# A long convolution with an MLP: three chunks of the next pass on GpSimd, raw weights ten steps ahead, the decay on the filter's first layer, MLP tiles moved

## The chip, the cores and the metric

The kernel runs on one core of a Trainium2 chip. The metric is the device time of one execution in microseconds, and of several runs the median. The engines appear under the profile's names: PE (TensorE: matmuls; its weight loads have a row of their own, PEld), DVE (VectorE), ACT (ScalarE), POOL (GpSimd) and SP (SyncE, which only issues DMAs here). Each engine executes its own instructions in the order in which they were issued to it; so does the queue of DMA issues of SP, and that of POOL. An instruction that waits holds up all that stand behind it on its engine.

## The reference

A long convolution of length 12480 (by FFT of twice the length) of u = x * v with a learned filter, gated by x, and then an MLP with a squared ReLU over all 49920 tokens.

```python
# x, v: (4, 12480, 128); pos_emb: (12480, 64); w1: (64, 64); w2: (64, 128); float32
h_filt = (np.maximum(pos_emb @ w1, 0.0) @ w2) * np.exp(-0.01 * pos)[:, None]
u = x * v
y = np.fft.irfft(np.fft.rfft(u, n=2*S, axis=1) * np.fft.rfft(h_filt, n=2*S, axis=0)[None], n=2*S, axis=1)[:, :S]
t = (x * y).reshape(B * S, D)                      # 49920 tokens of 128
r = np.maximum(t @ moe_w_in, 0.0)                  # (128, 2048), float64
out = ((r * r) @ moe_w_out).astype(np.float32)     # (2048, 128), float64
```

The decay exp(-0.01 * pos) underflows to zero beyond some thousands of positions, so the kernel computes only RF = 96 rows of 128 filter positions.

## The kernel before

The transform is done as two stages of matmuls with matrices of cosines and sines (sizes N1 = 90 and N2 = 128). The 128 channels are worked on in Q = 4 passes of 32 channels and all four batches. A pass `q` has two loops.

*First transforms* (`for c in range(NC)`, 20 steps). A chunk is 8 columns out of batch x channel. Chunks 0 to 15 carry data: `load_c` fetches x and v as [98, 1024] tiles (lines 164 to 168), `prep(c)` makes u on DVE from one product and an addition and a subtraction (lines 180 and 183). Chunks 16 to 19 carry the filter, which is fetched from DRAM tile `fd` and copied into u by ACT (line 189). `s1_quad` then does the matmuls of half a chunk (line 199) into one of two PSUM buffers, and ACT copies the result into the big SBUF tile P (line 202). In step c the kernel issues in this order: the load of chunk c + 5, the next piece of the weight conversion, in pass 0 the filter's layers, `prep(c + 2)`, and the two `s1_quad(c, .)`.

*The weight conversion.* The MLP's weights arrive as float64. `weights(i)` is a generator that handles one of eight column blocks: it fetches 512 KB of raw words into a single buffer (line 231), converts them by integer arithmetic on DVE into a high and a low float32 part (lines 237 to 256, 13 DVE instructions on 128x512 and an ACT copy) and stores them to DRAM tile `wd` (line 258). Each `next(part, 0)` runs it on to its next `yield`. A block is begun at steps 0 and 10 of each pass, so its raw load is issued one step ahead of the instructions that read it.

*The filter* (pass 0, steps 0 to 7; two pairs of groups a step). `filt(i)` is the first layer: a matmul of pos with w1 and a ReLU on ACT (line 134). `filt2(i)` is the second: 16 matmuls (line 143), a product with the decay on DVE (line 147, out of PSUM), then an addition on DVE and a subtraction on POOL (line 156) into the two `feo` tiles, of which there is one buffer each. `store_f` writes them to `fd` at the end of the step.

*Second transforms* (`for s in range(NS)`, 30 steps). `s2(z)` multiplies P with matrices `wt` that are fetched from DRAM, three steps ahead by `load_s(z + 3)` (lines 264 and 276). ACT copies the filter's part (line 280), DVE multiplies (line 284, PSUM by SBUF), POOL combines the products into y (lines 292 and 293). `i2(z - 2)`, two steps later, applies the inverse of the second stage to y (line 301); ACT and DVE take it out of PSUM and SP stores it to `cd` in DRAM (line 307). The list `todo` holds the transforms whose `i2` is outstanding: two are left at the end of the loop, and line 368 executes them after the first transforms of the next pass. Near the end of the loop (steps 24, 26, 28) the first three chunks of the next pass are loaded, and at steps 26 and 28 two of them prepared on DVE.

SBUF buffers: x, the products t and half of the filter tiles share five buffers with the tag "x"; v, y, the results `cs` and the other half of the filter tiles share five with the tag "v". u has four.

*The MLP stage* begins with `load3(0)` and `load3(1)`, which fetch a unit's columns of `cd`, its x and its inverse matrices (lines 395 to 405). `i1` does the inverse first stage, `tr` gates and transposes, and `h_chunk`, `g_chunk` and `o_chunk` do the two layers with weights split in high and low parts (`wi`, `wo`). `wi` and `w0` (the first unit's matrices) are fetched at the beginning of the last pass's second transforms, `wo` between `load3(0)` and `load3(1)`. The order of all instructions is the order of the program text (`tc.manual_schedule()`); the framework adds the waits that the data and the buffers need.

## Time and profile before

| | us |
|---|---|
| runs: median (lowest, highest) of 3 | 3218.98 (3217.07, 3224.23) |
| the profiled execution: its time | 3214.31 |
| the profiled execution: its span | 3212.4 |
| PE busy | 3037.3 (95%) |
| DVE busy | 2383.7 (74%) |
| ACT busy | 2107.2 (66%) |
| POOL busy | 704.1 (22%) |
| granted TensorE clock, mean | 0.977 |
| DMA, mean over the span | 91 GB/s |

The span is the part of the execution that the profile covers. An engine's busy time counts its instructions, not its waits. A row of the timeline has the start in us from the beginning of the span, the duration, the engine, the line, the operation with its output and inputs, and in brackets the idle time ahead of it and what ended that; SPq and POOLq are the queues of DMA issues. A row of the windows has a stretch, its length, the busy time of each engine with its number of instructions, the granted TensorE clock, the mean busy share of the 16 DMA engines and what they moved in GB/s.

### The profile page before, as it was taken

How to read it: one execution, taken by the hardware profiler on the slowest of the kernel's cores; microseconds unless marked ns; L12 is line 12 of the kernel's file. 1: busy time of each engine (PE TensorE's matmuls, PEld its weight loads, DVE VectorE, ACT ScalarE, POOL GpSimd, SP SyncE). 2: the span in 40 equal slices, each digit the busy share in tenths (PEclk: the TensorE clock that was granted, in tenths of full speed). 3: DMA queues.
4: the chain of work that ended last, by engine and by line, in shares of the span. 5: the costliest groups of instructions: out<-in, count | busy, mean ns of one | idle time of the engine just before them, and what ended most of it. 6: DMA issues, size and time to landing. Idle time of an engine off the chain costs nothing.

```text
span 3212.4 us, 41665 instructions
## 1 busy us (share of the span) xinstructions
PE 3037.3 (95%) x15338; PEld 2448.3 (76%) x15338; DVE 2383.7 (74%) x2765; ACT 2107.2 (66%) x2658; POOL 704.1 (22%) x598
## 2 busy tenths in 40 slices
PE   7696977879799999999999999999999999999999
PEld 4575766667688888888888888888888888888887
DVE  6596776759577777777777777777777777777776
ACT  2433434243577777777777777777777777777776
POOL 3160523406211112111111111111111111111210
PEclk8898989899899999999999999999999999999999
DMA  7576574766512122121122121222121221121200
GB/s 213 134 210 199 158 231 131 221 178 185 146 56 58 51 73 63 51 57 57 51 75 58 55 58 58 60 62 66 51 58 51 62 69 56 58 58 51 65 28 14
DMA packets 204266, 291.78 MB, mean 91 GB/s; under 512 B 13278, under 2 KB 129568, under 8 KB 203552
## 3 DMA queue, kind: packets, MB, share of 16 engines
q1 hardware_dynamic: 194704, 263.04, 28.6%
q0 software_dynamic: 9360, 26.10, 3.1%
q8 instruction: 121, 1.98, 0.3%
q14 instruction: 81, 0.66, 0.1%
HBM read 205.85 MB, written 83.23 MB: 90 GB/s over the span
## 4 chain that ended last, share of the span: by engine, by line
PE 85%; DMA 6%; DVE 6%; ACT 2%; issue 1%; POOL 0%; SPq 0%; DVEq 0%; POOLq 0%; ACTq 0%
PE psh L470 34%; PE pso L496 34%; PE psx L276 5%; PE psy L439 4%; PE psc L301 4%; DVE x L180 2%; DVE u L183 1%; PE pst L456 1%; PE pss L199 1%; DMA f<-fd 1%; DMA raw<-in_w_out_dram 1%; ACT u L189 1%; DMA cb<-cd 1%; DMA wt<-in_sw_dram 1%; DVE t L284 1%
## 5 line engine op out<-in xcount | busy, mean ns | idle before, releaser
L88 DVE TENSOR_TENSOR glo<-gt,ghi 128x1024 fp32r<-128x1024 f32 (+1 forms) x784 | 1090.2, 1390 | 60.6 <-PE psh L470 0.9
L473 ACT ACTIVATE rt<-psh 128x1024 f32<-128x1024 f32 (+1 forms) x784 | 800.0, 1020 | 433.7 <-PE psh L470 424.5
L482 DVE CAST ghi<-gt 128x1024 fp32r<-128x1024 f32 (+1 forms) x784 | 540.4, 689 | 502.9 <-ACT gt L480 502.4
L496 PE MATMUL pso<-ghi,wo 128*128 128x512 f32 (+1 forms) x3136 | 871.4, 395 | 0.0
L470 PE MATMUL psh<-xhi,wi 128*128 128x512 f32 (+1 forms) x3136 | 867.0, 398 | 0.9 <-ACT rt L473 0.4
L480 ACT ACTIVATE gt<-rt 128x1024 f32<-128x1024 f32 (+1 forms) x784 | 829.1, 1058 | 23.7 <-DVE glo L88 0.4
L496 PEld LDWEIGHTS pso<-ghi,wo 128*128 128x128 f32 x3136 | 591.2, 189 | 134.7
L470 PEld LDWEIGHTS psh<-xhi,wi 128*128 128x128 f32 x3136 | 579.9, 188 | 130.3 <-ACT rt L473 1.3
L88 POOL TENSOR_TENSOR clo<-ca,chi 128x512 fp32r<-128x512 f32 x126 | 225.1, 1787 | 1391.8 <-ACT chi L85 1369.1
L496 PE MATMUL pso<-glo,wo 128*128 128x512 f32 (+1 forms) x1568 | 504.8, 393 | 0.0
L470 PE MATMUL psh<-xlo,wi 128*128 128x512 f32 (+1 forms) x1568 | 488.8, 393 | 0.0
L199 PE MATMUL pss<-e_sb,u 98*64 98x180 f32 (+1 forms) x2560 | 249.7, 350 | 107.0 <-DVE u L183 84.6
L496 PEld LDWEIGHTS pso<-glo,wo 128*128 128x128 f32 x1568 | 294.9, 188 | 70.5
L470 PEld LDWEIGHTS psh<-xlo,wi 128*128 128x128 f32 x1568 | 294.8, 188 | 69.9
L199 PEld LDWEIGHTS pss<-e_sb,u 98*64 98x64 f32 (+1 forms) x2560 | 212.3, 152 | 143.7 <-issue 86.7
L202 ACT COPY P<-pss 128x720 f32<-128x720 f32 x160 | 125.2, 794 | 229.8 <-PE pss L199 229.8
L284 DVE TENSOR_TENSOR t<-psx,hs 128x768 f32<-128x768 f32 x240 | 218.2, 952 | 49.8 <-ACT hs L280 28.7
L276 PEld LDWEIGHTS psx<-P,wt 128*128 128x128 f32 x1440 | 212.5, 188 | 46.8 <-issue 11.7
L276 PE MATMUL psx<-P,wt 128*128 128x160 f32 x1440 | 221.9, 302 | 14.0 <-DMA wt<-in_sw_dram 6.6
L280 ACT COPY hs<-psx 128x192 f32<-128x192 f32 x240 | 65.1, 323 | 237.2 <-PE psx L276 233.8
L292 POOL TENSOR_TENSOR y<-t,t 128x384 f32<-128x384 f32 x120 | 120.3, 1002 | 377.2 <-DVE t L284 371.5
L88 POOL TENSOR_TENSOR clo<-cb,chi 104x512 fp32r<-104x512 f32 x126 | 165.8, 1316 | 114.1 <-ACT chi L85 114.0
(58 smaller groups left out, 1964.4 us busy)
## 6 DMA issues: line engine op xcount, KB each, us to landing
cd<-cs SPq DMA_DIRECT2D x120, 384.0 KB
cb<-cd SPq DMA_DIRECT2D x128, 208.0 KB
x<-in_xc_dram SPq DMA_DIRECT2D x64, 392.0 KB
v<-in_vc_dram SPq DMA_DIRECT2D x64, 392.0 KB
x<-in_x_dram SPq DMA_DIRECT2D x128, 196.0 KB
iwt<-in_iw_dram POOLq DMA_DIRECT2D x63, 392.0 KB, 3.4
out_dram<-os SPq DMA_DIRECT2D x48, 512.0 KB
wt<-in_sw_dram SPq DMA_DIRECT2D x120, 192.0 KB
```

What stands on the lines that cost most here:

```text
L88: eng.tensor_tensor(dst, src, hi.bitcast(F32), op=ALU.subtract)
L199: pe.matmul(pv[p, a], lhsT=u[:rows, 4 * h + a, p], rhs=e_sb[:rows, e : e + 2].rearrange("n c k -> n (c k)"), start=True, stop=True)
L202: act.copy(sl["P"][:, :, s : s + 4].rearrange("p m a t -> p a m t"), pv.rearrange("p a (m t) -> p a m t", t=2),)
L276: pe.matmul(xp[:, 3 * c + i, :SIG], lhsT=wt[:, i], rhs=sl["P"][:, c * (N1 // 2) + kp, :, t], start=True, stop=True)
L284: dve.tensor_tensor(t, xp[:, :, : B * QC].rearrange("p m (b d) -> p m b d", b=B), hs[:, c].rearrange("p r k d -> p (r k) d").unsqueeze(2). ...
L301: pe.matmul(cp[c], lhsT=f_sb[:, c], rhs=y[:, c], start=True, stop=True)
L439: pe.matmul(yp, lhsT=lhs, rhs=rhs, start=n == 0, stop=n == len(ops) - 1)
L470: pe.matmul(ps[:, j, :n], lhsT=wi[wp][:, f * 128 : (f + 1) * 128], rhs=bl[b][dp][:, j * n : (j + 1) * n], start=(wp, dp) == TERMS[0], stop ...
L473: act.activation(rt, ps[:, :, :n], AF.Relu)
L480: act.activation(gt, rt, AF.Square)
L482: dve.tensor_copy(hi, gt)
L496: pe.matmul(un["o"][j], lhsT=wo[tm[0]][:, f], rhs=g[tm[1]][:, j], start=f == 0 and tm == TERMS[0], stop=f == NF - 1 and tm == TERMS[-1])
```

## The change

1. *Chunks 0 to 2 of the next pass.* A new function `ahead` loads x and v into two buffers of its own (`a0`, `a1`, one each) and makes u on POOL in four instructions: two halves of the product, the addition, the subtraction. Its five parts run at every second step of the second transforms, beginning at steps 2, 10 and 18, in passes 0 to 2. The first transforms of passes 1 to 3 then begin with three chunks ready, and DVE prepares chunks 3 to 15.
2. *Raw weights.* The raw load is issued from POOL's queue instead of SP's, at step 9 of the first transforms for the block that begins at step 10, and before the loops or at step 16 of the second transforms for the block that begins at step 0. The conversion runs at steps 0 to 6 and 10 to 16, and the store at steps 9 and 19.
3. *Leftover `i2`.* The two outstanding transforms run in steps 1 and 2 of the next first transforms instead of behind them.
4. *Filter chunks.* Half of the copies into u go to DVE.
5. *Decay.* It is fetched together with pos, repeated over the 64 inner rows, and multiplied in with the ReLU in one DVE instruction; addition and subtraction follow on the first layer's output (DVE), and ACT copies the second layer's results out of PSUM into `feo`. POOL has no part in the filter any more.
6. *MLP tiles.* `wi`, `w0` and `wo` are fetched at steps 2, 6, 10 and 14 of the last pass's second transforms; the identity matrix is fetched at the beginning. A pad of 992 words moves addresses of the MLP stage, and the tile of constants is longer.

```diff
 load_f:
-                pt = wf.tile([2 * FO, G2 * RF], F32, tag="pos", name="pt", bufs=3)
+                pt = wf.tile([2 * FO, 2, G2 * RF], F32, tag="pos", name="pt", bufs=3)
 filt:
+            pt = sf.pop(("pos", i))
+            pe.matmul(ps, lhsT=w1_sb, rhs=pt[:, 0], start=True, stop=True)
+            hw = pt[:, 1]
+            dve.scalar_tensor_tensor(hw, ps, 0.0, hw, op0=ALU.max, op1=ALU.mult)
             h1 = wf.tile([2 * FO, G2, RF], F32, tag="h1", name="h1")
-            act.activation(h1.rearrange("p a b -> p (a b)"), ps, AF.Relu)
+            for e, op in enumerate((ALU.add, ALU.subtract)):
+                dve.tensor_tensor(h1[:, 2 * e : 2 * e + 2].rearrange("p a b -> p (a b)"),
+                                  hw[:, : 2 * RF], hw[:, 2 * RF :], op=op)
 filt2:
-                dve.tensor_tensor(ft, ps[h], win_sb[...], op=ALU.mult)
-                for e, op in enumerate((ALU.add, ALU.subtract)):
-                    (dve, pool)[e].tensor_tensor(fe, ft[:, :2], ft[:, 2:], op=op)
+                for e in range(2):
+                    act.copy(fe, ps[h][:, 2 * e : 2 * e + 2].rearrange("p j (q d) -> p j q d", q=Q))
 prep, filter chunks:
-                for e in range(2):
+                for e, copy in enumerate((dve.tensor_copy, act.copy)):
                     for h in range(2):
-                        act.copy(u[:RF, :, j : j + 32], ch["f", e, h][:, d : d + 8])
+                        copy(u[:RF, :, j : j + 32], ch["f", e, h][:, d : d + 8])
+        def ahead(q, k, i):
+            if i == 0:
+                for n, src in enumerate((xc, vc)):
+                    ch["a", n] = pre.tile([R1, 8 * N2], F32, tag=f"a{n}", name="xv"[n])
+                    sp.dma_start(ch["a", n], src[q, k])
+                return
+            x, v = ch["a", 0], ch["a", 1]
+            if i < 3:
+                h = slice((i - 1) * 4 * N2, i * 4 * N2)
+                pool.tensor_tensor(x[:, h], x[:, h], v[:, h], op=ALU.mult)
+                return
+            if i == 3:
+                ch["u", k] = s1.tile([R1, 8, N2], F32, tag="u", name="u")
+            e = i - 3
+            xr = x.rearrange("n (h s j) -> n h s j", h=2, s=8)
+            pool.tensor_tensor(ch["u", k][:, :, e * H2 : (e + 1) * H2], xr[:, 0], xr[:, 1], op=(ALU.add, ALU.subtract)[e])
 weights (float64 branch):
-                sp.dma_start(raw.rearrange("p c t -> p (c t)"), ...)
+                pool.dma_start(raw.rearrange("p c t -> p (c t)"), ...)
 the loop of passes:
-                for c in (3, 4):
+                for c in (3, 4, 5):
                     load_c(q, c)
                 for c in range(NC):
-                    if c + 5 <= NU:
+                    if 5 < c + 5 <= NU:
                         load_c(q, c + 5)
-                    if c % 10 == 0:
+                    if c % 10 < 7 or c % 10 == 9:
+                        next(part, 0)
+                    if c == 9:
                         part, wpart = weights(wpart), wpart + 1
-                    next(part, 0)
+                        next(part)
 ...
-                    if c + 2 < NC:
+                    if ready <= c + 2 < NC:
                         prep(c + 2)
 ...
+                    if todo and c:
+                        i2(todo.pop(0))
 ...
-                while todo:
-                    i2(todo.pop(0))
                 for s in range(NS):
 ...
-                    if q < Q - 1 and s in (26, 28):
-                        prep(s // 2 - 13)
-                    if q < Q - 1 and s in (24, 26, 28):
-                        load_c(q + 1, s // 2 - 12)
+                    if q < Q - 1:
+                        for k in range(3):
+                            if s in range(8 * k + 2, 8 * k + 11, 2):
+                                ahead(q + 1, k, s // 2 - 4 * k - 1)
+                        if s == 16:
+                            part, wpart = weights(wpart), wpart + 1
+                            next(part)
+                    elif s in (2, 6, 10, 14):
+                        i = s // 4 % 2
+                        if s < 10:
+                            sp.dma_start(wi[i].bitcast(F32), wd[0, i])
+                            pool.dma_start(w0[i], iw0[i])
+                        else:
+                            sp.dma_start(wo[i].rearrange("p c d -> p (c d)").bitcast(F32), wd[1, i])
+                ready = 3
 the MLP stage:
+    pad = ctx.enter_context(tc.tile_pool(name="p3pad", bufs=1, side="right"))
+    pad.tile([128, 992], F32, tag="pad", name="pad")
...
             load3(0)
-            for i in range(2):
-                sp.dma_start(wo[i].rearrange("p c d -> p (c d)").bitcast(F32), wd[1, i])
             load3(1)
```

More of the change, by code (lines that the diff above doesn't have):

```diff
@@ L79, in conv_moe @@
 @with_exitstack
-def conv_moe(ctx, tc, xc, vc, xg, pos, win, w1, w2, ew, fw, ident_d, sw, iw, iw0, w_in, w_out, out):
+def conv_moe(ctx, tc, xc, vc, xg, pos, w1, w2, ew, fw, ident_d, sw, iw, iw0, w_in, w_out, out):
     nc = tc.nc
@@ L131, in filt @@
             ps = psM.tile([2 * FO, G2 * RF], F32, tag="m1", name="psm1")
-            pe.matmul(ps, lhsT=w1_sb, rhs=sf.pop(("pos", i)), start=True, stop=True)
+            pt = sf.pop(("pos", i))
+            pe.matmul(ps, lhsT=w1_sb, rhs=pt[:, 0], start=True, stop=True)
+            hw = pt[:, 1]
+            dve.scalar_tensor_tensor(hw, ps, 0.0, hw, op0=ALU.max, op1=ALU.mult)
             h1 = wf.tile([2 * FO, G2, RF], F32, tag="h1", name="h1")
-            act.activation(h1.rearrange("p a b -> p (a b)"), ps, AF.Relu)
+            for e, op in enumerate((ALU.add, ALU.subtract)):
+                dve.tensor_tensor(h1[:, 2 * e : 2 * e + 2].rearrange("p a b -> p (a b)"),
+                                  hw[:, : 2 * RF], hw[:, 2 * RF :], op=op)
             sf["h", i] = h1
@@ L210, in conv_moe @@
         NUM = (0, 9, 21, 31, 254)
-        nums = const.tile([128, 24], U32, tag="num", name="nums")
+        nums = const.tile([128, 56], U32, tag="num", name="nums")
         def num(v):
@@ L222, in weights @@
                 raw = s1.tile([128, CW], F32, tag="raw", name="raw", bufs=1)
-                sp.dma_start(raw, dram_w[:, cols])
+                pool.dma_start(raw, dram_w[:, cols])
                 yield
                 split_hi(hi, raw)
-                yield
                 split_lo(dve, lo, raw, hi)
-                yield
+                for _ in range(6):
+                    yield
             else:
                 raw = s1.tile([128, CW, 2], U32, tag="raw", name="raw", bufs=1)
-                sp.dma_start(raw.rearrange("p c t -> p (c t)"), dram_w.bitcast(U32)[:, 2 * cols.start : 2 * cols.stop])
+                pool.dma_start(raw.rearrange("p c t -> p (c t)"), dram_w.bitcast(U32)[:, 2 * cols.start : 2 * cols.stop])
                 yield
@@ L319, in conv_moe @@
             load_f(1)
-            win_sb = load("win", [RF, N2], win)
             load_c(0, 0)
@@ L326, in conv_moe @@
             f_sb = load("f", [N2, 2, N2], fw)
+            ident = const.tile([R1, 112], F32, tag="ident", name="ident")[:, :R1]
+            sp.dma_start(ident, ident_d)
+            part, wpart = weights(0), 1
+            next(part)
             filt(0)
@@ L355, in conv_moe @@
                     psC = c1.enter_context(tc.tile_pool(name="psc", bufs=2, space=PSUM))
+                    early = ExitStack()
+                    pre = early.enter_context(tc.tile_pool(name="pre", bufs=1, side="right"))
                     for z in range(3):
@@ L358, in conv_moe @@
                 if q == Q - 1:
+                    early.close()
                     low.close()
@@ L384, in conv_moe @@
     w4 = ctx.enter_context(tc.tile_pool(name="p3w4", bufs=2))
-    wo = [w4.tile([128, NF, D], F32R, tag=f"wo{i}", name=f"wo{i}", bufs=1) for i in range(2)]
+    pad = ctx.enter_context(tc.tile_pool(name="p3pad", bufs=1, side="right"))
+    pad.tile([128, 992], F32, tag="pad", name="pad")
     io3 = ctx.enter_context(tc.tile_pool(name="p3io", bufs=2, side="right"))
@@ L506, in conv_moe @@
             load3(0)
-            for i in range(2):
-                sp.dma_start(wo[i].rearrange("p c d -> p (c d)").bitcast(F32), wd[1, i])
             load3(1)
@@ L623 @@
     k = _constants()
-    pos = _groups(pos_emb[None])
-    win = _groups(k["win"][None, :S, None])[..., 0]
+    pos, win = (_groups(a).transpose(0, 3, 2, 1).reshape(NG // 2, 2, -1, G2 * RF) for a in (pos_emb[None], k["win"][None, :S, None]))
+    pos, win = pos.reshape(NG // 2, 2 * FO, -1), np.repeat(win[:, :, 0], FO, 1)
     w_out = moe_w_out.reshape(NF, 128, D).transpose(1, 0, 2).reshape(128, DFF)
@@ L633 @@
         x=_pad_seq(x).reshape(B, R1, N2, Q, QC).transpose(2, 1, 3, 0, 4).reshape(N2, R1, W),
-        pos=pos.transpose(0, 3, 2, 1).reshape(NG // 2, 2 * FO, G2 * RF),
-        win=win.transpose(1, 0, 2).reshape(RF, N2),
+        pos=np.stack([pos, np.broadcast_to(win, pos.shape)], 2),
         w1=w1b, w2=np.concatenate([w2, w2]), ew=k["ew"], fw=k["fw"], ident=k["ident"], sw=k["sw"], iw=k["iw"], iw0=k["iw0"],
```

16 lines of the change are left out of this document (4 added, 12 removed).

## The prediction

> **What bounds the kernel now.** I read the busy time by stage first, the tile of the raw weights next, then the timeline of one pass and the windows of transfer rate. The stage table cuts the span at the instructions that begin a stage: the filter part of pass 0, the rest of its first transforms, then second and first transforms in turn, the change of stage, the MLP.
>
> ```profile
> span 3212.4 us, 41665 instructions
> ...
> L292 POOL TENSOR_TENSOR y<-t,t 128x384 f32<-128x384 f32 x120 | 120.3, 1002 | 377.2 <-DVE t L284 371.5
> ```
>
> ```profile
> core 0: us, PE busy (x) PEld busy (x) DVE busy (x) ACT busy (x) POOL busy (x), PEclk, DMA share, GB/s
> ...
> 21.10:94.88 73.78, 57.34 (x475) 39.42 (x474) 57.74 (x91) 17.86 (x28) 31.76 (x28) 0.87 0.78 209
> 94.88:148.57 53.69, 36.33 (x418) 31.97 (x417) 27.68 (x38) 28.99 (x43) 3.19 (x3) 0.86 0.51 136
> 148.57:239.77 91.20, 87.97 (x473) 71.53 (x473) 80.23 (x116) 29.64 (x88) 55.87 (x57) 1.00 0.69 189
> 239.77:334.36 94.59, 65.19 (x649) 54.91 (x649) 57.64 (x77) 41.49 (x60) 4.05 (x4) 0.86 0.59 171
> 334.36:425.45 91.09, 87.96 (x473) 71.45 (x471) 81.24 (x119) 29.73 (x89) 55.86 (x57) 1.00 0.72 200
> 425.45:521.46 96.01, 66.10 (x651) 56.17 (x651) 57.66 (x77) 41.50 (x60) 4.07 (x4) 0.82 0.58 169
> 521.46:611.89 90.43, 87.72 (x473) 71.29 (x472) 81.25 (x118) 29.64 (x88) 55.86 (x57) 1.00 0.72 201
> 611.89:708.69 96.80, 65.56 (x650) 55.27 (x650) 57.65 (x77) 41.45 (x60) 5.29 (x6) 0.84 0.61 170
> 708.69:800.52 91.83, 87.47 (x474) 71.52 (x472) 79.94 (x116) 29.67 (x89) 56.92 (x58) 1.00 0.72 208
> 800.52:832.60 32.08, 13.33 (x36) 7.26 (x37) 8.23 (x14) 3.72 (x7) 2.52 (x3) 0.68 0.81 216
> 832.60:3212.40 2379.80, 2372.86 (x10545) 1912.22 (x10543) 1787.15 (x1918) 1810.80 (x2044) 426.39 (x314) 1.00 0.20 57
> ```
>
> The last row is the MLP: TensorE 2372.9 of 2379.8 us, and the change takes no work from it. The second transforms are TensorE's too (88 of 91). The first transforms of passes 1 to 3 are nobody's: 94.6, 96.0 and 96.8 us, TensorE 65, DVE 58, ACT 41. Those three rows, 287.4 us together, are where the change can win.
>
> ```profile
>   DMA raw<-in_w_out_dram: 42.0, 4
>   DMA raw<-in_w_in_dram: 35.1, 4
> ```
>
> ```profile
> 250.33 0.42 SPq L231 DMA_DIRECT2D raw<-in_w_in_dram  x1
> ...
> 260.45 0.69 DVE L237 SCALAR_TENSOR_TENSOR cv<-raw,nums 128x512 uint32<-128x512 uint32 x1 [11.08 <-DMA raw<-in_w_in_dram]
> ...
> 261.79 1.22 DVE L180 TENSOR_TENSOR x<-x,v 98x1024 f32<-98x1024 f32 x1
> 263.03 0.32 SPq L168 DMA_DIRECT2D v<-in_vc_dram  x1
> 263.04 1.29 DVE L183 TENSOR_TENSOR u<-x 98x512 f32<-98x512 f32 x2
> ...
> 263.85 0.29 PEld L199 LDWEIGHTS pss<-e_sb,u 98*64 98x64 f32 x2 [10.53 <-issue]
> ```
>
> The raw weights stop DVE eight times, 77.1 us in all: asked for at 250.33, one step ahead of their use, landed at 260.45. The preparation of a chunk (1.22 + 1.29 = 2.51 us) stands behind them in DVE's order and TensorE behind that (10.53 idle). The v load at 263.03 went out only when the product had freed a buffer: two of the five "v" buffers hold the y of the last two second transforms until line 369, behind the whole chunk loop.
>
> ```profile
> 239.77:302.00 62.23, 41.58 (x417) 34.96 (x416) 40.97 (x53) 21.15 (x27) 4.05 (x4) 0.86 0.80 234
> ```
>
> ```profile
> 253.00:260.00 7.00, 0.76 (x5) 0.24 (x2) 0.00 (x0) 0.76 (x1) 0.00 (x0) 0.74 0.94 290
> ```
>
> Transfers ran at 234 GB/s on average until the filter tiles landed, and at 290 while everything waited for them: a limit stands close behind the waits.
>
> **The change part by part.** *First transforms, passes 1 to 3.* Three chunks come ready from GpSimd, so DVE prepares 13: 13 x 2.51 = 33 us. The 26 weight instructions stay, 26 x 0.69 = 18 at most; two i2 move in, four additions of about 0.5, 2 us. Half of each filter chunk's copies comes to DVE, 8 of 256 elements; two of 512 took 1.29, so 0.3 to 0.65 each, 4 us. The last real chunk is ready after 33 + 14.5 (21 weight instructions) + 2 = 49.5 us; five chunks of TensorE follow.
>
> ```profile
> 131.49 2.66 PE L199 MATMUL pss<-e_sb,u 98*64 98x180 f32 x32 [1.31 <-ACT P L202]
> ...
> 320.09 2.32 ACT L189 COPY u<-f 96x256 f32<-96x256 f32 x4
> 322.26 1.50 ACT L202 COPY P<-pss 128x720 f32<-128x720 f32 x2
> ```
>
> A chunk costs TensorE 2.66 us (20 x 2.66 = 53 in a pass, 56 with the two i2). A filter chunk cost ACT 2.32 + 1.50 = 3.82, more than TensorE; with half the copies gone it is 1.16 + 1.50 = 2.66, level. So DVE's floor is 49.5 + 5 x 2.66 = 62.8. For the transfers: 13 chunks of 2 x 98 x 4 KB (10.4 MB), the filter tiles 1.6, raw, stores and cd 1.9, together about 13.9 MB. At 290 the filter would be there after 48 us, at 234 after 59, then four chunks and a tail, 12 us. I take 265, between them: 52 + 12 = 64, and 65 with a start in which chunk 3 is asked for only at the pass's beginning. Bounds 63 and 72. Term: 287.4 - 3 x 65 = **92 us less** (71 to 98).
>
> The raw load's wait goes for 10 steps; late next is chunk data or the filter tiles. On GpSimd's queue the load no longer stands behind SP's blocked v load, and in the first transforms nothing is queued behind it there. It reads the buffer's freedom, given four steps earlier. If that cover went, the old 10 us would return at each of eight places.
>
> *Second transforms, passes 0 to 2.* In even steps GpSimd gets one more instruction of 512 elements, twelve a pass. By y's 1002 ns for 384 it costs 1.34 us.
>
> ```profile
> 207.16 1.85 PE L276 MATMUL psx<-P,wt 128*128 128x160 f32 x12
> ...
> 212.44 0.59 SPq L307 DMA_DIRECT2D cd<-cs  x1
> ...
> 214.60 1.00 POOL L292 TENSOR_TENSOR y<-t,t 128x384 f32<-128x384 f32 x1 [1.01 <-DVE t L284]
> 214.79 1.45 PE L301 MATMUL psc<-y,f_sb 128*128 128x384 f32 x4
> ...
> 239.89 1.97 POOL L293 TENSOR_TENSOR y<-t,t 128x384 f32<-128x384 f32 x1
> ```
>
> GpSimd's idle 1.01 ahead of 214.60 tells that the y of the transform at 207.16 was done at 213.59; the matmul that uses it begins at 214.79. So y has 1.2 us of slack, beside the 1.0 of idle time. An instruction of up to 2.2 us is therefore free; 1.34 is, 1.34 x 1.97 = 2.64 (the doubling that y shows at 239.89 beside a DVE instruction) would cost 0.4 each. I take nothing, 0 to 5 us a pass. The raw load at step 16 adds one issue on that queue, less than the slack.
>
> The six loads of a pass have a price of their own, in SP's order:
>
> ```profile
> 225.34 0.35 SPq L168 DMA_DIRECT2D x<-in_xc_dram  x1
> ...
> 226.47 0.40 SPq L264 DMA_DIRECT2D wt<-in_sw_dram  x1
> ...
> 232.18 1.92 PE L276 MATMUL psx<-P,wt 128*128 128x160 f32 x12 [1.07 <-DMA wt<-in_sw_dram]
> ```
>
> The transform weights asked for behind a chunk landed 5.7 us later, and TensorE lost 1.1. After the change the loads of chunks 1 and 2 (steps 10 and 18) also have to wait for the buffer that GpSimd's last subtraction of the chunk before, in the same step, still reads: that ends 7.8 us behind the step's transform (y done after 6.4, plus 1.34), and SP arrives there at 5.9 (the store at 212.44 is issued 5.3 behind 207.16 and takes 0.59). SP stands still with the next weights and the next store behind it, so the stall is some 2.9 us for these two: 1.1 + 2 x 2.9 = 7 a pass. Before, the tail with its two preparations cost 2.1 to 2.9 a pass (91.20, 91.09 and 90.43 against 88.3, the last pass without its own stall): 7.8 together. Term: 21 - 8 = **13 us more** (0 to 18).
>
> *Pass 0.* In a step of two pairs of groups DVE's eight instructions (four of 512 elements, four of 256) become six (two of 384, four of 192), GpSimd's four go, and ACT gets eight copies for two relus.
>
> ```profile
> 84.12 4.67 POOL L156 TENSOR_TENSOR feo<-ft 96x256 f32<-96x256 f32 x4 [4.81 <-DMA fd<-feo]
> ...
> 93.61 1.40 POOL L156 TENSOR_TENSOR feo<-ft 96x256 f32<-96x256 f32 x2 [4.81 <-DMA fd<-feo]
> ```
>
> ```profile
> 332.63 0.48 ACT L303 COPY ci<-psc 128x384 f32<-128x384 f32 x1
> ```
>
> One step there is a ring through the single feo buffers: 4.67 of GpSimd, 4.81 of store, 9.5 in all. After it is 8 copies of 256 (0.48 for 384, about 0.37 each, 3 us) with 1.5 of second-layer matmuls between, 4.5, and the same 4.8: 9.3. But pos comes with a copy of the decay, 0.39 MB more a step, 2.37 MB instead of 1.98; at 209 GB/s 11.3 us, at 290 8.2. I take 10, half a us more in each of seven steps, and 1.5 us for the fuller start: 5 us later at the end of the filter part. Behind it (53.69 us now) the raw wait and the slow filter chunks go: TensorE's 13 chunks are 35 us, and DVE's weight instructions of two loads (18) beside six preparations (15) let about 39 of it remain. Term: 5 - 15 = **10 us less** (20 less to 3 more).
>
> *Last pass.* wi and wo (1 MB each) and w0 are spread over steps 2 to 14.
>
> ```profile
> 719.62 1.93 PE L276 MATMUL psx<-P,wt 128*128 128x160 f32 x12 [2.98 <-DMA wt<-in_sw_dram]
> ```
>
> Two MB at once cost 3 us. Each load alone is larger than a chunk (1.1 for 0.8 MB); with w0's 0.4 MB 2.3, without 1.3: 7 against 3, **4 us more** (0 to 8). What they free is the change of stage: 2 MB of wo less between the two first loads of cd, 7 us of transfer at 290, of which only the part ahead of the first MLP chunk counts.
>
> ```profile
> ACT chi L85 <- DMA cb<-cd: 1.2, 2, 0.7
> ```
>
> ACT waits 1.2 us there after 832.6, and the first pair's own 10 us would shorten by some 3: **4 us less** (0 to 8). The pad and the longer const tile move addresses alone: nothing.
>
> Sum: -92 + 13 - 10 + 4 - 4 = -89. The profiled execution took 3214.31 (span 3212.4 and 1.9 around it), so the sum gives 3125 for it. The median of the runs shown, 3218.98, lies 4.7 higher; I forecast 3130 for the median.
>
> **The rivals.** *Transfers set the first transforms.* If 234 GB/s is what this mixture gives, a pass takes 59 + 12 = 71 to 72, and pass 0 comes out 3 later: -71 + 3 + 13 + 4 - 4 = -55, 3164. For it: 0.94 of the engines busy at 253. Against: in the same rows SP was blocked by v. The Trainium skill, "DMA: Bandwidth & Descriptors", section "Issuing engines are not separate DMA queues", says that DMAs started by different engines run on the same 16 engines and interleave, so that GpSimd's queue saves issue time and adds no bandwidth. By that rule the raw load's move makes nothing faster but its being early, and the case stays open at 0.25.
>
> *All hides.* Loads of chunks stall nothing more than now, DVE's floor of 63 holds, pass 0 wins 20, and the change of stage 6: -98 - 20 - 6 = -124, 3095. For it: 6 us of lead for the weights; against: the 1.1 at 232.18. Chance 0.2.
>
> *GpSimd becomes the bound, slower than before.* Thirty-six extra instructions must together lose over 89 + 13 us: beyond the free 2.2 us each, 2.8, so from 5.0 us each it is slower; at 6 us 3219 + 36 x 3.8 - 102 = 3254. For it: 1.97 for one y. Against: beside t, which reads PSUM, y takes 1.00. The Trainium skill, "SBUF — State Buffer", section "Who interferes with whom", calls the port pair of DVE and GpSimd an exclusive lock and puts a DVE instruction with two SBUF inputs in contention with a GpSimd one that reads SBUF. By that rule the 1.97 belongs to u's two SBUF inputs, which the second transforms no longer have; the trace agrees. Chance 0.03; gains eaten to within 0.2% 0.02.
>
> **How the numbers follow.** The sum has 0.5. The range goes from the second rival to the first, 3094 to 3166; the sum's own is 3110 to 3150. A change of 0.2%, 6 us, is about what can be told from none: faster 0.95, within it 0.02, slower 0.03.
>
> **What would show it.** First transforms of passes 1 to 3 near 65 us each, no DVE wait for raw, DVE's last preparation near 50 us into the pass; second transforms of 92 to 96 with TensorE waiting for wt behind steps 10 and 18; y at 1.00 and GpSimd's new instructions near 1.34; filter steps near 10 us. Wrong, if chunk or filter loads stop DVE for more than 5 us a pass, if the new instructions take over 2.2 us, or if the MLP's 2379.8 moves.

## The result and the profile after

The changed kernel takes 3099.45 us (median of four runs, 3098.57 to 3113.79) against 3220.35 of the kernel before, measured beside it (3217.07 to 3224.23): a ratio of 0.9635, 95% interval 0.9604 to 0.9665. The forecast was 3130 with a range of 3094 to 3166. The time lies inside, but two misses cancel in part in it: one term was 23 us too large, and a part that had been put down as nothing brought 49.5.

The profiled execution took 3098.57, 115.74 less than the profiled one of before. Its span and TensorE's row, from the head of the page:

```profile
span 3096.6 us, 41700 instructions
...
PE 2983.8 (96%) x15338; PEld 2432.2 (79%) x15338; DVE 2351.0 (76%) x2754; ACT 2105.8 (68%) x2674; POOL 719.8 (23%) x610
```

The windows of the changed kernel, cut as those of before: the filter part of pass 0, the rest of its first transforms, second and first transforms in turn, the last pass's second transforms with the change of stage, the MLP.

```profile
core 0: us, PE busy (x) PEld busy (x) DVE busy (x) ACT busy (x) POOL busy (x), PEclk, DMA share, GB/s
23.95:92.95 69.00, 53.92 (x475) 37.69 (x474) 40.77 (x75) 28.69 (x72) 0.53 (x1) 0.90 0.91 260
92.95:133.71 40.76, 34.47 (x418) 30.69 (x417) 25.34 (x39) 26.49 (x39) 0.00 (x0) 0.92 0.57 164
133.71:226.43 92.72, 88.00 (x473) 71.44 (x473) 78.37 (x113) 29.64 (x88) 71.94 (x71) 1.00 0.71 202
226.43:303.73 77.30, 66.09 (x650) 51.85 (x649) 55.90 (x81) 38.05 (x52) 3.39 (x4) 0.91 0.73 202
303.73:399.26 95.53, 89.72 (x472) 72.57 (x473) 78.29 (x113) 29.70 (x88) 71.91 (x71) 0.98 0.69 196
399.26:470.54 71.28, 62.60 (x649) 50.43 (x648) 55.51 (x81) 38.03 (x52) 3.39 (x4) 0.95 0.71 220
470.54:564.89 94.35, 89.70 (x473) 72.73 (x473) 78.32 (x113) 29.55 (x88) 71.89 (x71) 0.98 0.70 199
564.89:635.05 70.16, 61.60 (x649) 50.48 (x648) 55.50 (x81) 38.02 (x52) 3.41 (x4) 0.95 0.74 223
635.05:766.33 131.28, 104.85 (x508) 81.15 (x509) 87.13 (x127) 33.36 (x95) 60.47 (x63) 0.90 0.69 198
766.33:3096.60 2330.27, 2323.91 (x10545) 1908.16 (x10543) 1785.38 (x1918) 1811.83 (x2044) 431.71 (x314) 1.00 0.20 58
```

Against the windows of before, and with the forecast's terms beside them:

| stage | before | after | difference | forecast |
|---|---|---|---|---|
| all up to the end of pass 0's first transforms | 148.57 | 133.71 | -14.9 | -10 |
| second transforms, passes 0 to 2 | 272.7 | 282.6 | +9.9 | +13 |
| first transforms, passes 1 to 3 | 287.4 | 218.7 | -68.7 | -92 |
| last second transforms and change of stage | 123.9 | 131.3 | +7.4 | 0 |
| MLP | 2379.8 | 2330.3 | -49.5 | 0 |
| sum | | | -115.8 | -89 |

The MLP has the same 10545 matmuls at the same clock, 1.00, and TensorE is busy without a break in both. Its matmuls became shorter. Two groups of the page of before, then the same two of after (the last numbers ahead of the second bar are the sum in us and the mean of one in ns):

```profile
L496 PE MATMUL pso<-ghi,wo 128*128 128x512 f32 (+1 forms) x3136 | 871.4, 395 | 0.0
L470 PE MATMUL psh<-xhi,wi 128*128 128x512 f32 (+1 forms) x3136 | 867.0, 398 | 0.9 <-ACT rt L473 0.4
```

```profile
L504 PE MATMUL psh<-xhi,wi 128*128 128x512 f32 (+1 forms) x3136 | 851.6, 393 | 0.5 <-ACT xhi L85 0.4
L530 PE MATMUL pso<-ghi,wo 128*128 128x512 f32 (+1 forms) x3136 | 851.9, 388 | 0.0
```

These two save 19.5 and 15.4 us, the two like groups with xlo and glo another 13.5. A chunk of a layer is six such matmuls. From start to start (worked out from the trace), the next one follows by 227 ns (median) at each of the six places of after, and by 228 to 241 before, differing with the place.

### The profile page after: what moved, and what is told of

Its sections match the earlier page's. It is cut to its first block, busy times and chain, and to the rows that moved or that the text cites. A ratio compares the mean times of both kernels' runs of the same rounds, so it can differ in the third digit from the quotient of the medians.

```text
span 3096.6 us, 41700 instructions
## 1 busy us (share of the span) xinstructions
PE 2983.8 (96%) x15338; PEld 2432.2 (79%) x15338; DVE 2351.0 (76%) x2754; ACT 2105.8 (68%) x2674; POOL 719.8 (23%) x610
## 4 chain that ended last, share of the span: by engine, by line
PE 75%; DMA 1%; ACT 0%; DVE 0%; issue 0%; POOL 0%; SPq 0%; ACTq 0%; DVEq 0%
PE psh L504 34%; PE pso L530 34%; PE psy L473 5%; PE pst L490 1%; DMA cb<-cd 0%; DMA ca<-cd 0%; DMA cd<-cs 0%; ACT rt L507 0%; ACT gt L514 0%; DVE ghi L516 0%; DVE gx L477 0%; POOL clo L88 0%; ACT xhi L85 0%; ACT chi L85 0%; DVE glo L88 0%
## 5 line engine op out<-in xcount | busy, mean ns | idle before, releaser
L504 PE MATMUL psh<-xhi,wi 128*128 128x512 f32 (+1 forms) x3136 | 851.6, 393 | 0.5 <-ACT xhi L85 0.4
L530 PE MATMUL pso<-ghi,wo 128*128 128x512 f32 (+1 forms) x3136 | 851.9, 388 | 0.0
L530 PE MATMUL pso<-glo,wo 128*128 128x512 f32 (+1 forms) x1568 | 497.6, 388 | 0.0
L504 PE MATMUL psh<-xlo,wi 128*128 128x512 f32 (+1 forms) x1568 | 482.5, 389 | 0.0
L217 PE MATMUL pss<-e_sb,u 98*64 98x180 f32 (+1 forms) x2560 | 237.6, 335 | 31.3 <-DVE u L183 15.4
L217 PEld LDWEIGHTS pss<-e_sb,u 98*64 98x64 f32 (+1 forms) x2560 | 196.8, 144 | 73.0 <-ACT P L220 32.3
L294 PE MATMUL psx<-P,wt 128*128 128x160 f32 x1440 | 226.4, 306 | 25.7 <-DMA wt<-in_sw_dram 18.2
```

Of the source, the lines that this page charges most:

```text
L217: pe.matmul(pv[p, a], lhsT=u[:rows, 4 * h + a, p], rhs=e_sb[:rows, e : e + 2].rearrange("n c k -> n (c k)"), start=True, stop=True)
L294: pe.matmul(xp[:, 3 * c + i, :SIG], lhsT=wt[:, i], rhs=sl["P"][:, c * (N1 // 2) + kp, :, t], start=True, stop=True)
L504: pe.matmul(ps[:, j, :n], lhsT=wi[wp][:, f * 128 : (f + 1) * 128], rhs=bl[b][dp][:, j * n : (j + 1) * n], start=(wp, dp) == TERMS[0], stop ...
L530: pe.matmul(un["o"][j], lhsT=wo[tm[0]][:, f], rhs=g[tm[1]][:, j], start=f == 0 and tm == TERMS[0], stop=f == NF - 1 and tm == TERMS[-1])
```

## The experiments

**The MLP: is it the addresses, and whose?** The instructions of the stage are the same, so only the places of its tiles are left as a cause. In the compiled programs the change moves them in two ways. The pad shifts all working tiles (xhi, xlo, ghi, glo and what ACT and DVE use) by 3968 bytes: from 224 bytes above a multiple of 256 to 96 above one. The longer const tile and the new order of the weight tiles shift wi from 32 above a multiple of 256 to 96; wo is at 96 in both. The inverse matrices and the x of the units move with the second of these too.

*Without the pad.*

```diff
-    pad = ctx.enter_context(tc.tile_pool(name="p3pad", bufs=1, side="right"))
-    pad.tile([128, 992], F32, tag="pad", name="pad")
```

> The changed kernel without the pad: the MLP's working tiles go back to the addresses that they had before (3968 bytes further up), the weights wi and wo stay where the change put them. In the changed kernel the MLP stage took 2330.3 us, before 2379.8. If the place of the working tiles (what TensorE streams and what the other engines write) makes the difference: the stage is back at 2380, matmuls of 512 columns follow one another at 229 to 241 ns, and the whole takes 3098.6 + 49.5 = 3148. Rival, the place of the weights: the stage stays at 2330 and the whole at 3099. Rival, both: something between, 3124 if they share it evenly.

Measured: 3148.74 us, ratio to before 0.978 (0.976 to 0.9799). The window of its MLP stage:

```profile
773.46:3149.30 2375.84, 2369.56 (x10545) 1914.40 (x10543) 1787.46 (x1918) 1810.95 (x2044) 426.28 (x314) 1.00 0.20 57
```

45.6 of the 49.5 us are back, and matmuls follow one another at 231 to 232 ns (median) at each of the six places.

*The kernel before with the pad alone* (the same two lines added to it).

> The kernel before with the pad of 992 words alone. If the place of the working tiles makes the MLP's difference: the stage takes 2330 in place of 2379.8, nothing else moves, and the whole is 3219 - 49.5 = 3170. Rival, the place of the weights: 2380 and 3219.

Measured: 3177.8 us, ratio 0.987 (0.9854 to 0.9887). Its MLP window, and two groups of its page:

```profile
833.40:3174.60 2341.20, 2333.95 (x10545) 1908.02 (x10543) 1785.77 (x1918) 1811.68 (x2044) 431.39 (x314) 1.00 0.20 58
```

```profile
L472 PE MATMUL psh<-xhi,wi 128*128 128x512 f32 (+1 forms) x3136 | 856.8, 395 | 1.2 <-ACT rt L475 0.7
L498 PE MATMUL pso<-ghi,wo 128*128 128x512 f32 (+1 forms) x3136 | 853.5, 389 | 0.0
```

The pad alone brings 38.6 us. Most of the 10.9 that are missing lie in the first layer: psh is at 395 ns where the changed kernel has 393 (5.2 us in this group, another 3.5 in the one with xlo), while pso, whose weights are at 96 in both, is down to 389. That speaks for the place of wi where the working tiles are well placed. Where they are badly placed the other moves bring 4 us (2379.8 against 2375.8), but not in the first layer alone: in the run without the pad pso with ghi takes 868.4 us and psh with xhi 864.7, 3.0 and 2.3 less than before. "Both" is what the two runs show, with the larger part the pad's; that the smaller part is wi's is argued for the first layer and not tried by itself.

*A pad of 384 bytes, and one of 128.* Only the number of words in the pad's line is changed, to 96 and to 32.

> The changed kernel with a pad of 96 words (384 bytes) in place of 992 (3968 bytes). The pad of 992 puts the MLP's working tiles 96 bytes above a multiple of 512; without it they lie 480 above one; this pad puts them at 96 again, 3584 bytes from where the change has them. MLP stage: 2330.3 us with 992 words, 2375.9 with none. If only the place within 512 bytes counts: 2330. If the place within 1024 or more counts, or what lies where on a larger scale: some other value, 2376 for no effect at all.

> The changed kernel with a pad of 32 words (128 bytes): the MLP's working tiles lie 352 bytes above a multiple of 512 and 96 above a multiple of 256, as the change has them within 256 but not within 512. If only the place within 256 bytes counts: the MLP stage takes 2330. If the place within 512 counts: another value, between 2330 and 2376 or beyond.

```profile
772.84:3102.80 2329.96, 2323.97 (x10545) 1908.07 (x10543) 1785.56 (x1918) 1811.80 (x2044) 431.74 (x314) 1.00 0.20 58
```

```profile
780.67:3110.70 2330.03, 2323.95 (x10545) 1907.81 (x10543) 1785.63 (x1918) 1811.68 (x2044) 431.69 (x314) 1.00 0.20 58
```

Both give the whole gain, 2330.0 us (one execution each, of 3104.59 and 3112.46 as a whole; what that has above the changed kernel lies outside the MLP). 128 bytes do what 3968 do: what the three pads have in common is the place within 256 bytes (96; without a pad 224). One place within 256 against one other is all that was tried; which of the tiles that move together matters, those that TensorE streams or those that ACT and DVE write meanwhile, stays open.

**The first transforms: DVE's chain, or transfers?** They took 77.3, 71.3 and 70.2 us. The forecast had 65, from transfers at 265 GB/s a little above DVE's floor of 63, and 71 to 72 by the rival in which transfers at 234 GB/s set them.

*No conversion on DVE.* The 13 DVE instructions of a weight block go, and `act.copy(hi, wh)` and `act.copy(lo, wh)` from the raw high words take their place, so the weights are not the reference's.

> The changed kernel without the integer conversion of the weights on DVE: the raw words are still fetched and a block still stored, but ACT copies the raw high words into both halves, so the weights are not those of the reference. This takes 26 DVE instructions, 18.6 us, out of each pass and leaves every transfer. The first transforms of passes 1 to 3 took 77.3, 71.3 and 70.2 us in the changed kernel. If the transfers set them (13 chunks, the filter tiles, raw words and stores, at 260 to 297 GB/s with the DMA engines 0.93 to 0.94 busy): they stay at 70 to 77. If DVE's chain sets them: they fall to the next limit, TensorE's 56 with its two inverse transforms, plus a start of 4, so 60 each, 39 us less in the three.

*No v.* For chunks 3 to 15 of passes 1 to 3, v is not fetched and DVE multiplies x by itself, so u is not the reference's.

```diff
-                for n, src in enumerate((xc, vc)):
+                for n, src in enumerate((xc, vc)[: 2 if q == 0 else 1]):
...
-                dve.tensor_tensor(x, x, v, op=ALU.mult)
+                dve.tensor_tensor(x, x, ch.pop((c, 1), x), op=ALU.mult)
```

> The changed kernel without the load of v for chunks 3 to 15 of passes 1 to 3: DVE squares x in its place, so u is not the reference's. DVE's instructions stay as many and as long, 5.2 of about 15.6 MB of transfers go from each of these first transforms. If transfers set them: they fall from 77.3, 71.3 and 70.2 to DVE's own chain, 48.9 of work to chunk 15 and 13.3 for five chunks of TensorE, 63 to 65 each, and the spread of 7 us between passes goes. If DVE's chain sets them: only the waits for v go (6.1, 3.5 and 3.9 us): 71, 68 and 66.

The windows of the three first transforms without the conversion, and then without v:

```profile
223.87:296.41 72.54, 61.23 (x649) 50.53 (x648) 38.83 (x55) 38.95 (x54) 2.95 (x4) 0.93 0.71 216
391.35:463.14 71.79, 61.15 (x649) 49.56 (x648) 38.91 (x55) 38.92 (x54) 2.94 (x4) 0.95 0.70 218
558.30:634.08 75.78, 62.08 (x649) 49.27 (x648) 38.96 (x55) 38.76 (x54) 2.95 (x4) 0.95 0.72 207
```

```profile
228.06:295.60 67.54, 59.65 (x649) 49.52 (x648) 55.40 (x81) 37.68 (x52) 3.40 (x4) 0.97 0.53 154
388.94:456.23 67.29, 59.55 (x649) 49.36 (x649) 55.39 (x81) 37.65 (x52) 3.39 (x4) 0.97 0.53 155
548.65:616.43 67.78, 59.91 (x649) 49.48 (x648) 55.38 (x81) 37.64 (x52) 3.40 (x4) 0.97 0.52 154
```

The first takes 17 us of DVE's 55.5 away, and the three stages together take 220.1 (218.7 in the changed kernel): nothing. The second takes a third of the bytes away and leaves DVE's work: 202.6, all three within half a microsecond of one another. So what goes with v's transfers is 9.8, 4.0 and 2.4 us, and the spread with it. But 67.5 is left without them, above the 63 to 65 that were expected there, and in the second and third of the stages the result is as near to the other expectation, of DVE's chain. The changed kernel's second stage shows why. What DVE waited for there, and then in the same stage without the conversion (us in all, times, longest):

```profile
DVE x L180 <- DMA v<-in_vc_dram: 3.5, 1, 3.5
```

```profile
DVE x L180 <- DMA v<-in_vc_dram: 13.5, 7, 7.1
```

The end of DVE's last preparation in that stage, in the changed kernel and then without v:

```profile
452.60 1.29 DVE L183 TENSOR_TENSOR u<-x 98x512 f32<-98x512 f32 x2
```

```profile
441.15 1.29 DVE L183 TENSOR_TENSOR u<-x 98x512 f32<-98x512 f32 x2
```

Behind its one wait, near the head of the stage, DVE works on without a break until chunk 15 is ready, 54.6 us in; 16.7 follow. Without v chunk 15 is ready 53.5 us in and 13.8 follow. So 67.5 is DVE's chain with the chunks of TensorE behind it, and late data come on top: little in this stage, most in the first. The two limits lie close together. Without the conversion the transfers alone hold the stages where they were; without v DVE's chain does, a few microseconds lower. The whole took 3095.3 and 3080.52 us.

*What the spread is.* One pair of windows shows it best. It is from the kernel of the next part, whose first transforms have the changed kernel's instructions: 40 us of its first and of its last, from 4 us behind their start, and the two stages whole.

```profile
227.07:295.93 68.86, 59.11 (x649) 48.27 (x649) 55.39 (x81) 37.60 (x52) 3.40 (x4) 1.00 0.73 227
...
547.95:626.75 78.80, 64.12 (x650) 50.04 (x649) 55.83 (x81) 37.79 (x52) 3.38 (x4) 0.94 0.74 199
...
231.07:271.07 40.00, 34.87 (x368) 27.79 (x366) 35.49 (x50) 19.63 (x26) 0.60 (x1) 1.00 0.94 306
551.95:591.95 40.00, 34.45 (x334) 25.97 (x332) 31.85 (x44) 17.91 (x24) 0.60 (x1) 0.96 0.94 252
```

The DMA engines were 0.94 busy in both, yet moved 306 GB/s in one and 252 in the other, and the stage took 68.9 and 78.8 us. In the changed kernel's own three it is 260, 297 and 287 GB/s for 77.3, 71.3 and 70.2. The rate changes from stage to stage of one execution, with no fixed order between passes; why, no run here tells. It also limits what the later comparisons can tell: the same first transforms added up to 218.7, 223.3, 219.5 and 227.0 us in the changed kernel and the three variants of its pad.

**The wait for wt in the second transforms.** TensorE waited 18.2 us for wt, 12.0 of it in passes 0 to 2. The forecast had SP stand still at the chunk loads with wt behind. The changed kernel's timeline around step 10 of pass 0:

```profile
169.86 1.30 POOL L208 TENSOR_TENSOR u<-x 98x512 f32<-98x512 f32 x1
...
171.19 0.34 SPq L197 DMA_DIRECT2D x<-in_xc_dram  x1
171.58 0.38 SPq L197 DMA_DIRECT2D v<-in_vc_dram  x1
172.05 0.35 SPq L282 DMA_DIRECT2D wt<-in_sw_dram  x1
...
177.30 1.92 PE L294 MATMUL psx<-P,wt 128*128 128x160 f32 x12 [1.79 <-DMA wt<-in_sw_dram]
```

GpSimd's subtraction ends at 171.16, SP issues the load 0.03 later, and the wt behind it is asked for at 172.05; TensorE lost 1.79.

```diff
-                    sp.dma_start(ch["a", n], src[q, k])
+                    pool.dma_start(ch["a", n], src[q, k])
```

> The changed kernel with the loads of chunks 0 to 2 for the next pass issued from GpSimd's queue instead of SP's. TensorE waited for wt in passes 0 to 2 for 12.0 us in nine places: 0.75, 0.77 and 0.33 behind the first chunk's load, 1.13 to 2.05 behind the second's and third's. If SP's standing still at the loads of the second and third chunk (they wait for the subtraction that still reads the buffer) makes those longer, all nine become like the first, some 0.6 each: 12.0 - 5.6 = 6.4, and the whole is 3099 - 6 = 3093. Rival: the wt loads are late because 0.8 MB of chunk data goes ahead of them on the same DMA engines, whichever queue asks; then the waits stay at 12 and the whole at 3099. Rival on the other side: GpSimd's queue, standing at the load, delays y; then TensorE waits for y and the whole is some us over 3099.

Measured: 3096.12 us, ratio 0.9628 (0.9601 to 0.9654), not told apart from the changed kernel's 0.9635. The stages tell more. What waited for wt, in the changed kernel and then with the loads on GpSimd's queue (us in all, times):

```profile
  PE psx L294: 18.2, 13
```

```profile
  PE psx L294: 5.7, 3
```

The waits of passes 0 to 2 are gone altogether, the first chunk's too, which had been put down to the transfer alone. TensorE waits 6.1 us for y in exchange (twelve times), so the second transforms take 91.7 each, 7.5 less in sum. The order in the queue was the cause; the bytes, which are the same, were not. Seven executions shown here have these second transforms as they are in the changed kernel: their sum is 279.1 to 283.0, with 11 to 12.4 us of waits for wt. The two with the loads on GpSimd's queue have 275.1 and 274.5, and no such wait.

**The raw weights: lead or queue?** The block is begun at steps 0 and 10 again, and the early issues at step 16 and ahead of the loops are gone; the load stays on GpSimd's queue.

```diff
-                    if c % 10 < 7 or c % 10 == 9:
-                        next(part, 0)
-                    if c == 9:
+                    if c % 10 == 0:
                         part, wpart = weights(wpart), wpart + 1
-                        next(part)
+                    next(part, 0)
...
-                        if s == 16:
-                            part, wpart = weights(wpart), wpart + 1
-                            next(part)
```

> The changed kernel with the raw weights asked for one step ahead of their use again, but still on GpSimd's queue. If the lead is what took the raw wait away: a load that lands some 7 us after its issue meets DVE after one step of 3.7 us or less, so DVE waits 4 to 7 us at each of the six places in passes 1 to 3 and at the two of pass 0, TensorE behind it, and the whole is 3099 + 8 x 5 = 3140. Rival: the queue did it, since on SP's the load stood among blocked chunk loads; then DVE waits under 2 us each and the whole is 3099 to 3110. Rival: the transfers set the first transforms anyway, so DVE's waits return in full and the stage still takes 70 to 77 us: 3099 to 3105.

Measured: 3116.46 us, ratio 0.9683 (0.9664 to 0.9703). Between the expectations, and for a reason that none of them had. One pass in its timeline:

```profile
406.16 0.59 POOL L248 DMA_DIRECT2D raw<-in_w_out_dram  x1
414.18 0.69 DVE L254 SCALAR_TENSOR_TENSOR cv<-raw,nums 128x512 uint32<-128x512 uint32 x1 [9.14 <-DMA raw<-in_w_out_dram]
...
431.94 0.53 POOL L248 DMA_DIRECT2D raw<-in_w_out_dram  x1 [25.19 <-DVE cv L267]
450.42 0.68 DVE L254 SCALAR_TENSOR_TENSOR cv<-raw,nums 128x512 uint32<-128x512 uint32 x1
```

DVE waits 9.14 us for the block of step 0, but not for that of step 10: its load goes out at 431.94, as soon as DVE has released the buffer, 18 us ahead of its use. GpSimd has nothing else to do in these stages, so its queue stands at the load long before the step in which the text has it. In the text this block's load stands one step ahead of its use before, in the changed kernel (steps 9 and 10) and here alike; what lead it has beyond that is the queue's doing. Three waits came back in all, 27.6 us, in place of eight with 77.1. So on GpSimd's queue the lead in the text matters for the block of step 0 alone (three times); the queue does the rest.

**Chunks 0 to 2 on DVE again.** In place of the calls of `ahead`:

```diff
+                        if s in (26, 28):
+                            prep(s // 2 - 13)
+                        if s in (24, 26, 28):
+                            load_c(q + 1, s // 2 - 12)
```

> The changed kernel with chunks 0 to 2 of the next pass as before: loaded at steps 24, 26 and 28 of the second transforms, 0 and 1 prepared there by DVE, 2 in step 0 of the first transforms. The second transforms of passes 0 to 2 go back from 92.7, 95.5 and 94.3 us to the 91.2, 91.1 and 90.4 of before: 9.8 less. If transfers set the first transforms: they stay, since chunks 3 to 15 are loaded at the same places, and the whole is 3099 - 10 = 3089: the part on GpSimd is a loss. If DVE sets them: each is 2.5 longer for chunk 2 and the whole is 3097.

Measured: 3104.4 us, ratio 0.9645 (0.9619 to 0.967). The second transforms came back as expected (90.9, 90.9 and 91.3, 9.4 less), the first ones took 232.9 in place of 218.7, more than either expectation has (their transfers moved 289, 270 and 262 GB/s; how much of the 14 us is theirs is not shown). The whole is above both expectations and not told apart from the changed kernel: no run shows that the preparation on GpSimd gains anything, and it may be worth a few microseconds either way.

**Three attempts to gain on it.** *Chunk 3 loaded earlier*, at step 28 of the second transforms:

> The changed kernel with the load of chunk 3 issued at step 28 of the second transforms of the pass before, instead of at the head of the first transforms. DVE's first preparation in passes 1 to 3 waited 4.6, 3.5 and 3.9 us for that load. If DVE's chain sets the first transforms, they shorten by these 12.0 us, less what two more loads cost at step 28 (about one wt wait of 1 to 2 us a pass): 3099 - 12 + 5 = 3092. Rival: transfers set them (0.91 to 0.98 of the DMA engines busy in 406 to 448); then what is loaded earlier is waited for later, at the filter tiles, and the whole stays at 3099 or rises by the wt waits to 3104.

Measured: 3101.0 us, 0.9631 (0.9609 to 0.9653). First transforms of 71.8, 73.4 and 71.9, 217.0 in sum: the rival's "stays", since the bytes only move.

*The filter tiles in the middle.* They are the last to land, and 17 us follow in which the DMA engines have little to do. The changed kernel, second of these passes:

```profile
453.11 1.33 ACT L189 COPY u<-f 96x256 f32<-96x256 f32 x2 [1.05 <-DMA f<-fd]
454.33 1.45 ACT L220 COPY P<-pss 128x720 f32<-128x720 f32 x2
...
455.17 1.14 PE L217 MATMUL pss<-e_sb,u 98*64 98x180 f32 x12 [2.43 <-ACT P L220]
```

```diff
+                if q:
+                    order = [0, 1, ..., 12, 16, 17, 13, 18, 14, 19, 15]
+                    fetch = [0, 1, ..., 12, 16, 13, 14, 15]
...
-                        load_c(q, c + 5)
+                        load_c(q, fetch[c + 5])
...
-                        prep(c + 2)
-                    s1_quad(c, 0)
+                        prep(order[c + 2])
+                    s1_quad(order[c], 0)
```

> The changed kernel with another order of chunks in the first transforms of passes 1 to 3: the filter tiles are fetched behind chunk 12, and the chunks are worked on as 0 to 12, 16, 17, 13, 18, 14, 19, 15. Work and transfers are the same. If transfers set these stages and what lies behind the last landing is paid in full: today the filter tiles land last, at 453.0, 54 us into the second of these passes, and 17 us of four filter chunks and a half follow with the DMA engines idle; with a data chunk last there follow 2.5 us of preparation and some 4 of TensorE and ACT, so a pass takes 61 to 64 in place of 77.3, 71.3 and 70.2, and the whole 3099 - 30 = 3069. Rival: DVE's chain, 49 for the chunks and 3 for the filter's copies, with the waits that it has on the way, ends where it ends now or later, and the passes stay over 69: 3090 or more.

Measured: 3104.59 us, 0.9643 (0.9628 to 0.9658); first transforms of 76.4, 73.4 and 75.0. The second of them:

```profile
447.81 0.64 ACT L189 COPY u<-f 96x256 f32<-96x256 f32 x1 [5.35 <-DMA f<-fd]
...
450.46 9.31 PE L217 MATMUL pss<-e_sb,u 98*64 98x180 f32 x96 [5.76 <-ACT P L220]
...
461.56 1.22 DVE L180 TENSOR_TENSOR x<-x,v 98x1024 f32<-98x1024 f32 x1
```

The stage began at 400.82 (the changed kernel's at 399.26). The filter tiles land 47 us into it, 7 earlier than in the changed kernel, but ACT's copies of them now stand three steps earlier in its order, and with them the copies that empty TensorE's buffers: ACT waits 5.35 and TensorE 5.76, in place of 1.05 and 2.43. The last chunk is prepared 61 us into the stage and another 12.7 follow, since TensorE is behind by then. The expected gain turned into a longer wait in ACT's order.

*Both*, the order and the chunk loads on GpSimd's queue:

> The order of the run before this one, and the loads of chunks 0 to 2 issued from GpSimd's queue, as in the run that took 7.5 us from the second transforms of passes 0 to 2. If the two parts do not touch each other: second transforms of 91.7 each, first transforms of 61 to 64, the whole 3099 - 30 - 7 = 3062. Rival: transfers that start earlier in the second transforms' end meet the head of the first ones; then less than the sum, 3069.

Measured: 3098.63 us, 0.9621 (0.9602 to 0.964): second transforms of 91.9, 91.2 and 91.5, as in the run with the loads alone, first transforms of 79.8, 71.8 and 76.3 at 242, 289 and 265 GB/s. No version tried is shown to be faster than the changed kernel as a whole. The loads on GpSimd's queue are the one part that gained in its own stage in both runs that have it (7.5 and 8.1 us).

## Why the prediction was right, and where it was not

**The MLP** is the step that failed outright: "The pad and the longer const tile move addresses alone: nothing." Addresses alone were worth 49.5 us, 43% of the whole gain; by the run without it the pad has 45.6 of them. The forecast named this as a sign against it ("if the MLP's 2379.8 moves"), but gave it no chance. Without it the other terms give 66.3 less, and the profiled execution would have taken 3148 where the sum had 3125. The range holds both times, but at its two ends: the first transforms brought 23 us less than their term, the last pass took 7 more than its own, and a gain that the sum did not have more than made up for both. That they cancel is luck.

**First transforms, passes 1 to 3**: the raw waits went, as forecast, and DVE's conversion no longer stops, but the term was mis-sized. "I take 265, between them: 52 + 12 = 64" was too low in both parts. The filter landed 59.6, 53.8 and 55.0 us into the three stages, 56 in the mean, and 17.7, 17.4 and 15.2 followed, not 12, because TensorE still had a chunk and a half of data ahead of the filter's four, and waited 2.3 to 3.7 us for ACT's copies behind the landing. The rate was near what was assumed; the bytes were not: 223 GB/s over 70.16 us are 15.6 MB, not 13.9. DVE's floor was too low as well: chunk 15 was ready 58.5, 54.6 and 55.2 us in, and 53.5 to 54.0 even without v, where "The last real chunk is ready after 33 + 14.5 (21 weight instructions) + 2 = 49.5 us". DVE first has some 2 us of the pass before to finish and waits 2.4 to 2.8 for chunk 3, so the floor is 67.5 and not 62.8. Of the 23 us, 16 go with v's transfers (218.7 against 202.6) and the rest is the floor (202.6 against 3 x 65). The rival's price of 71 to 72 was right to 1 or 2 us in two of the three stages, not in the first; its cause, which had been given 0.25, is the larger part of the miss and not all of it. One more sign that the forecast named against itself came: chunk loads stopped DVE for 6.7 us in the first of these passes, over the 5 (3.5 and 3.9 in the others).

**The rule on queues.** The Trainium skill, "DMA: Bandwidth & Descriptors", section "Issuing engines are not separate DMA queues", was drawn on for saying that GpSimd's queue adds no bandwidth. No run here shows more bandwidth by a change of the queue: with the chunk loads on GpSimd's queue 40 us of each of the first transforms moved 306, 304 and 252 GB/s, with them on SP's 260, 297 and 287. But the forecast concluded that the move "makes nothing faster but its being early", as if the steps in the text made it early. On an idle engine the queue itself did that for every second block.

**Second transforms, passes 0 to 2**: +9.9 for +13. The cause was as told, SP standing at the chunk loads (171.16, 171.19, 172.05), with waits of 1.1 to 2.1 us for the second and third chunk in place of 2.9, and 0.3 to 0.8 for the first. GpSimd's new instructions took 1.30 where 1.34 was forecast, and y stayed at 1.00:

```profile
L208 POOL TENSOR_TENSOR u<-x x18: 1290/1302/1316, 163.9 to 559.3; 98x512 f32<-98x512 f32 x18
```

So the rival in which GpSimd becomes the bound fell with it.

**Pass 0**: -14.9 for -10. The start ahead of the filter part took 2.9 us more (23.95 for 21.10), where 1.5 had been put down. The rest of it came out as worked out (40.8 for 39). The filter part did not get longer but 4.8 us shorter, 69.0 for 73.8: its DMA engines were 0.91 busy and moved 260 GB/s, not the 209 of before, so its larger pos cost less than assumed. That transfers set it fits these figures; no run tried it.

**The last pass**: +7.4 for +4 - 4. The second transforms, up to the last matmul of the inverse, and the same of before:

```profile
635.05:738.92 103.87, 94.79 (x480) 75.33 (x480) 81.58 (x118) 30.60 (x90) 59.90 (x62) 0.97 0.70 205
```

```profile
708.69:805.04 96.35, 90.58 (x481) 72.87 (x479) 82.62 (x120) 30.63 (x91) 58.87 (x60) 1.00 0.72 207
```

They are 7.5 longer: waits for wt of 6.2 in place of 3.0, and TensorE busy 4.2 longer at a granted clock of 0.97 in place of 1.00. What taking wo away from the change of stage should have freed, 4 us, was not there. The first matmul of the MLP stage, after and before:

```profile
754.17 1.17 PE L473 MATMUL psy<-chi,iw0t 128*98 128x512 f32 x2 [15.25 <-DMA cb<-cd]
```

```profile
820.09 1.17 PE L439 MATMUL psy<-chi,iw0t 128*98 128x512 f32 x2 [15.05 <-ACT chi L85]
```

TensorE stands still for 15 us in both. The first loads of cd were issued ahead of wo before, too, and from the first of them to this matmul it took 10.9 us after (issued at 743.31) and 10.7 before (at 809.39). So wo had not been in their way.

## What to carry to other kernels

Where a stage is one long run of matmuls, a change of addresses alone is a change to be costed: a pad was worth 1.5% here (45.6 us), 128 bytes did as much as 3968, and one run with another pad shows it. Where the DMA engines are over 0.9 busy, count the bytes of the stage from the profile (rate times length) before costing instructions, and look behind the last landing for what still has to follow it. Where two limits lie close together, taking one away shows only the distance to the other: take away each in turn, and look at what the engine waits for, before calling one of them the cause. A load that may wait for a buffer belongs on the queue of the engine that releases the buffer, or on one that has nothing else behind it; and in an engine's order, a copy that waits for a transfer holds up the copies that empty a neighbour's buffers.

## What was not expected of the hardware

Matmuls of 128x512 that TensorE executes back to back follow one another at 227 ns or at up to 241 (medians), at the same granted clock of 1.00, by the place of the MLP's tiles in SBUF: 227 with the working tiles and both weights 96 bytes above a multiple of 256 (at three distances, 128, 384 and 3968 bytes from the slow place), 231 to 232 with the working tiles at 224, and 228 to 241 with those at 224 and wi at 32. The DMA engines, 0.93 to 0.94 busy, moved between 252 and 306 GB/s in stages of the same instructions (242 at 0.95 in one with another order of chunks). For neither did a run show the mechanism.
